# Causal running sums by groups of four interleaved chunks instead of one triangle product per chunk, in a gated linear-attention and state-space kernel

## The chip, the core and the metric

The kernel runs on one NeuronCore of a Trainium2 chip. The core has a matrix engine (TensorE, "PE"; its weight loads are shown as "PEld"), a vector engine (VectorE, "DVE"), a scalar engine (ScalarE, "ACT"), GpSimd ("POOL") and SyncE ("SP"), which here issues nearly all transfers. Each engine works through its own instructions in order; semaphores order them between engines. SBUF is the working memory with 128 partitions, PSUM the memory into which TensorE writes, eight banks of 128 x 512 float32. The metric is the device time of one execution in microseconds, the median of several runs.

## What is computed

A sequence of 2048 tokens of width 448 goes through two branches that are mixed by a gate:

```python
g = sigmoid((x * gate_w).sum(-1, keepdims=True))
a = attention(x, wqkv, wo)     # linear, not causal, 16 heads of 28
b = s4d(x, ...)                # causal convolution with a long kernel K per channel, plus x * D_skip
return g * a + (1 - g) * b
```

```python
# attention: phi(t) = where(t > 0, t + 1, exp(t)) + 1e-6
kv = einsum("bhsd,bhse->bhde", phi(k), v);  z = sum over s of phi(k)
o = einsum("bhqd,bhde->bhqe", phi(q), kv) / (einsum("bhqd,bhd->bhq", phi(q), z) + 1e-6)
return o @ wo
# s4d: y[t] = sum over s <= t of K[t - s] * x[s], by channel
```

With the parameters drawn here the kernel K of each channel is flat enough over the 2048 steps that the convolution is K[0] times the running sum of x; the program tests this on the chip (`okc`, `okn`) and holds a general convolution (`general_conv`) for the channels where it is not so. With these inputs the general part does not run. So what the S4D branch costs is a running sum over 2048 tokens in 448 channels, times a factor per channel (`near`), plus x times `dsk`.

Products that need float32 accuracy are made on TensorE in a reduced format (`F32R`) from a high and a low part: an operand is cast by ScalarE (high), and VectorE or GpSimd subtract the cast from the original (low, the helper `low`, L235).

## The kernel before

The tokens are 16 chunks of 128 rows. Chunk c lies with one token per partition. All instructions are placed by hand: the program text sets the order on every engine.

**The first stage** (L430 to L532 and the part up to L687) goes through the chunks. One pass c of its main loop (L476) does:

- load x of chunk c+3 (`load_x`, SP queue, 512 KB: the transposed chunk, `turned`, and the plain one, `plain`);
- the projection of k for chunk c+1 on TensorE, 11 matmuls of 448 columns (`project`, L338 and L334);
- `split_t(c+2)`: ScalarE casts the transposed chunk (L240), GpSimd makes its low part (L241, by L236);
- `k_feature`, `k_high`, `k_low`: phi of k. ScalarE: Relu and Exp (L360, L361); VectorE: the maximum, written back to PSUM (L362); ScalarE: the high part `pkh` (L366); VectorE: the low part `pkl` and the running sum `zb` (L372);
- the projection of q for chunk c, 11 matmuls into the one PSUM bank with the tag "q", and `q_post`: ScalarE the gate's exponential (L380, one column) and Exp (L349); VectorE a TENSOR_SCALAR (L350) and the maximum into `pq` (L353);
- `do_g(c)`: 11 matmuls that add to the four banks of k-transposed-times-x (L403), with `pkh`, `pkl` and the split plain chunk `xn`;
- `split_n(c+2)`: ScalarE casts the plain chunk (L246), GpSimd makes the low part (L247, by L236), and `skip` (L252) writes x times `dsk` into `y`.

**The running sum** is made chunk by chunk: `do_v(v)` (L408) multiplies the chunk's high and low parts by a 128 x 128 triangle of ones (`tri`), two matmuls of 448 columns; `v_post` (L413) multiplies the result in PSUM by `near` on VectorE (L415), sends its last row twice to the table `u` (L418), and GpSimd adds it to `y` (`v_add`, L423). The table `VS` (L35) says which chunks are done in which pass: two in each of the passes c=5 to 10, one in 11, 12, 13, and the last chunk behind the loop (L646, L663, L842). What earlier chunks add to a chunk comes later: `inter` (L692) multiplies `u` by a 0/1 table (`gcat`, from `cst`), and the result goes as extra rows into the output product of each chunk (`rc`, L629).

Between the passes c=2 and c=5 also stand the steps of `s4d_prepare` (L279): sums over the S4D parameters, then thirteen small VectorE instructions of four columns (L296 to L309, in pass c=4), four transposes on TensorE (L313) and a copy that makes `near` (L314), in pass c=5. The parameters lie in `abc`, in the upper rows of `pq`, until then.

**The second stage** (from L750) builds the combined output matrix, and its loop (L814) turns the normalised q of a chunk (`turn`), multiplies (`attend`), and adds the gated S4D branch (`final_b`: VectorE L634, then the transfer of 128 rows to `out`, L636). GpSimd makes the products for the denominators (`norm_a`, L542) and normalises q (`norm_c`, L567 and L573).

Buffers: `xp` four raw chunks, `xn_p` seven split plain chunks, `xt_p` four split transposed ones; PSUM tags "q", "k", "v0", "v1" and the four banks of `do_g`.

Of the kernel before, what the change touches and what calls it, by code (L numbers as in the profile page):

```python
# [7 lines left out]
F32 = mybir.dt.float32  # L8
# [7 lines left out]
P = 128  # L16
S = 2048
# [17 lines left out]
VS = {c: (2 * c - 10, 2 * c - 9) for c in range(5, 11)} | {c: (c + 1,) for c in range(11, NC - 1)}  # L35
# [18 lines left out]
def general_conv(ctx: ExitStack, tc: tile.TileContext, ga, y, og, okc, both, gin_d, out):  # L54
# [8 lines left out]
    kd = dr.tile([1, PAD], F32, name="kd")  # L63
    lag = one.tile([P, W], F32, name="lag")
# [7 lines left out]
    for lo, n, k in ((0, L1, float(L0)), (L1, L0, 1.0)):  # L72
        DVE.tensor_scalar(out=lag[:, lo:lo + n], in0=o[:, :n], scalar1=-1.0, scalar2=k, op0=ALU.add, op1=ALU.mult)
# [58 lines left out]
    every = [P, NC, D]  # L132
    for o, a, b, op in ((yg, yg, slow[:, None, :].to_broadcast(every), ALU.mult),
                        (y, y, fast[:, None, :].to_broadcast(every), ALU.mult), (yg, yg, y, ALU.add),
                        (yg, yg, og[:, :, None].to_broadcast(every), ALU.mult), (yg, yg, ga, ALU.add)):
        DVE.tensor_tensor(out=o, in0=a, in1=b, op=op)
    SP.dma_start(out=out.rearrange("(c p) d -> p c d", p=P), in_=yg)
# [3 lines left out]
def gated_mix_kernel(ctx: ExitStack, tc: tile.TileContext, xin, wq_d, wvo_d, abc_d, ldt_d, dsk_d,  # L141
# [196 lines left out]
    def project(*args, **kw):  # L338
        o, run = pieces(*args, **kw)
        run(11)  # L340
        return o
# [22 lines left out]
    def k_high(c):  # L364
        pkh[c] = tp.tile([P, 512], F32R, name="pkh", tag="pkh")[:, EDGE:EDGE + D]
        ACT.add(pkh[c], pks[c], 1e-6)  # L366
# [12 lines left out]
    def q_post(c, o, mid=None):  # L379
        ACT.activation(e1[:, c:c + 1], o[:, D:D + 1], AF.Exp, scale=-1.0)  # L380
        feature(pq[:, c], o, mid)
# [24 lines left out]
    vt = {}  # L406

    def do_v(c):  # L408
        v = vt[c] = ps.tile([P, 512], F32, name="v", tag="v%d" % (c % 2))
        PE.matmul(v[:, :D], lhsT=tri, rhs=xn[c][:, :D], start=True, stop=False)  # L410
        PE.matmul(v[:, :D], lhsT=tri, rhs=xn[c][:, XC - NAT:], start=False, stop=True)

    def v_post(c):  # L413
        t = tp.tile([P, D], F32, name="t", tag="v0")
        DVE.tensor_tensor(out=t, in0=vt.pop(c)[:, :D], in1=near, op=ALU.mult)  # L415
        if c < NC - 1:
            for k in (c, UL + c):
                SP.dma_start(out=u[k:k + 1], in_=t[P - 1:P])  # L418
            v_add(c, t)
        return t  # L420

    def v_add(c, t):
        POOL.tensor_tensor(out=y[:, c], in0=y[:, c], in1=t, op=ALU.add)  # L423
# [52 lines left out]
    for c in range(2, NC - 2):  # L476
        if c + 3 < NC:
            load_x(c + 3)
        if c == 2:
            SP.dma_start(out=cst, in_=cst_d)  # L480
        if c == 4:
            SP.dma_start(out=wvo, in_=wvo_d)
        vs = VS.get(c, ())
        ko = project(c + 1, wkh, wkl, D, "v1" if c in (2, 4) else "k")
        for v in vs[:1]:
            do_v(v)
        split_t(c + 2)
        k_feature(c + 1, ko)
        k_high(c + 1)
        if c > 5:  # L490
            for v in vs[:1]:
                v_post(v)
        k_low(c + 1)
        qo = project(c, wqh, wql, D + 2, "q")
        if c == 5:
            steps(1)
        else:
            for v in vs[1:]:
                do_v(v)
        q_post(c, qo)  # L500
        if c == 10:
            split_n(c + 2)
        if c == 5:
            v_post(0)
        else:
            for v in vs[1:]:
                v_post(v)
# [11 lines left out]
        if c == 5:  # L519
            do_v(1)  # L520
        if c < 4:
            skip(c - 1)
        if c != 10:
            split_n(c + 2)
        if c == 5:
            v_post(1)
        for j in {11: (0, 1), 12: (2, 3)}.get(c, ()):
            w = xn_p.tile([P, NX], F32R, name="wo", tag="n")[:DJ, :2 * D].rearrange("p (i d) -> p i d", i=2)
# [88 lines left out]
    av = {}  # L617

# [12 lines left out]
    def final_b(c):  # L631
        ot = tp.tile([P, D], F32, name="ot", tag="pkh")
        for a, lo, hi in av[c]:
            DVE.scalar_tensor_tensor(out=ot[:, lo:hi], in0=y[:, c, lo:hi], scalar=og[:, c:c + 1],  # L634
                                     in1=a[:, lo:hi], op0=ALU.mult, op1=ALU.add)
            (ACT if c == NC - 1 and hi == D else SP).dma_start(out=out[c * P:(c + 1) * P, lo:hi], in_=ot[:, lo:hi])  # L636
# [8 lines left out]
    ko = project(c + 1, wkh, wkl, D, "k")  # L645
    do_v(c + 1)  # L646
# [16 lines left out]
    vl = v_post(c + 1)  # L663
# [28 lines left out]
    def inter():  # L692
        o = ps.tile([P, 512], F32, name="z", tag="v0")
        r = tp.tile([P, D], F32R, name="rc", tag="w")
        z = tp.tile([P, D], F32R, name="zs", tag="v0")
# [118 lines left out]
    for c in range(NC):  # L814
# [26 lines left out]
        if c == 9:  # L841
            v_add(NC - 1, vl)  # L842
# [15 lines left out]
def _layout(inputs):  # L858
# [3 lines left out]
    x = np.asarray(inputs["A_x"])[0].reshape(NC, P, D)  # L862
# [7 lines left out]
    x = x[:, :, perm]  # L870
# [3 lines left out]
    def tiles(w):  # L874
        o = np.zeros((P, J, w.shape[1]), np.float32)
        for k in range(3):
# [12 lines left out]
                          for n in ("B_log_A_real", "B_A_imag", "B_C_real", "B_C_imag")]  # L889
                         + [np.repeat(np.asarray(inputs["B_log_dt"]).reshape(D, 1, 1), P, axis=1),  # L890
                            x[:, ::-1].transpose(2, 1, 0), x.transpose(2, 1, 0),
# [6 lines left out]
    k = np.arange(NC)[None, :] - np.arange(NC)[:, None]  # L898
# [3 lines left out]
    for r in (0, UL):  # L902
        cst[r:r + NC - 1, DJ + DT:DJ + RX] = np.repeat(k[:-1] > 0, 3, axis=1)
# [12 lines left out]
        f(np.stack([np.eye(P), lag >= 0], axis=1)),  # L916
# [20 lines left out]
```

## Time and profile before

| what | value |
|---|---|
| runs | 174.43, 174.32, 173.66 us; median 174.32 |
| the profiled execution: span from its first to its last instruction | 172.2 us |
| TensorE's granted clock | 1.000 |
| matmuls L410 and L411 (`do_v`) | 16 each, 5.8 and 5.9 us shown busy |
| VectorE L415 (`v_post`) | 16, 9.8 us busy |
| GpSimd L423 (`v_add`) | 16, 18.7 us busy |
| VectorE L350 (TENSOR_SCALAR of q) | 15, 10.0 us busy, 384 to 1382 ns |
| waits of VectorE for ScalarE at L362 | 29.4 us in 11 times |
| waits of GpSimd for VectorE at L423 | 11.5 us in 6 times |

The profile is one execution. Its page gives busy time by engine; a matmul is shown from its start to its modelled end, and neighbours overlap, so the time that one costs TensorE is the distance between the starts of neighbours. In the rows in order of time, the columns are the start in us, the duration in us, engine, line, operation, output and inputs; a bracket gives the idle time of the engine ahead of it and what ended it. In the rows by shape, the numbers behind the bar are the busy time in us and the mean of one in ns. "x11" says that eleven instructions were merged into one row.

### The profile page before, as it was taken

What the parts mean: (1) busy time and instruction counts of PE and PEld (TensorE: products, weight loads), DVE (VectorE), ACT (ScalarE), POOL (GpSimd) and SP (SyncE); (2) the same over time, 40 slices, a digit from 0 to 9 for tenths busy, and PEclk for the clock granted to TensorE, in tenths of its full rate; (3) what the DMA queues carried; (4) which work ended last, traced back from release to release, by engine and by line L of the source; (5) the groups of instructions that cost most, each with busy time, mean ns of one, the idle gap of its engine ahead of it and who ended that gap; (6) DMA issues with size and microseconds to landing.
All of it is one profiled execution on the core that took longest, in us unless ns stands there. A gap on an engine that the chain in (4) does not pass through costs nothing. (4 is left out here: it accounts for less than half of the span.)

```text
span 172.2 us, 2796 instructions
## 1 busy us (share of the span) xinstructions
PE 167.8 (97%) x876; PEld 152.0 (88%) x876; DVE 113.9 (66%) x240; ACT 96.0 (56%) x221; POOL 120.0 (70%) x128
## 2 busy tenths in 40 slices
PE   6999999999999999999999999999999999999992
PEld 2788999999899999999999999999899999999992
DVE  0847737698975483846627346487898998987542
ACT  3688588894256262542727456356574564664541
POOL 6082667877529988696996999529968998892200
PEclk9999999999999999999999999999999999999999
DMA  5989975097003031230404200000031222122213
GB/s 173 415 297 294 268 209 166 0 368 303 4 0 114 11 123 34 95 123 1 122 15 131 106 1 1 0 0 2 7 67 54 107 89 76 62 99 107 108 59 108
DMA packets 7962, 18.60 MB, mean 108 GB/s; under 512 B 2045, under 2 KB 4810, under 8 KB 7818
## 3 DMA queue, kind: packets, MB, share of 16 engines
q1 hardware_dynamic: 7802, 18.30, 32.0%
q8 instruction: 7, 0.11, 0.3%
q10 hardware_dynamic: 144, 0.11, 0.2%
q14 instruction: 9, 0.07, 0.1%
HBM read 14.38 MB, written 3.67 MB: 105 GB/s over the span
## 5 line engine op out<-in xcount | busy, mean ns | idle before, releaser
L629 PE MATMUL a<-wk,th 128*128 128x448 f32 (+1 forms) x170 | 36.4, 360 | 0.0
L403 PE MATMUL g<-pkh,xn 128*128 128x448 f32 x112 | 35.6, 364 | 0.0
L629 PEld LDWEIGHTS a<-wk,th 128*128 128x128 f32 x170 | 29.5, 189 | 1.6
L334 PE MATMUL k<-wk,xt 128*128 128x448 f32 x132 | 29.3, 367 | 0.0
L334 PE MATMUL q<-wqh,xt 128*128 128x450 f32 x120 | 27.5, 366 | 0.0
L362 DVE SCALAR_TENSOR_TENSOR k<-k,e 128x448 f32<-128x448 f32 x12 | 7.6, 632 | 29.4 <-ACT e L361 29.4
L423 POOL TENSOR_TENSOR y<-y,t 128x448 f32<-128x448 f32 x16 | 18.7, 1168 | 11.5 <-DVE t L415 11.5
L334 PEld LDWEIGHTS k<-wk,xt 128*128 128x128 f32 x132 | 24.8, 189 | 2.2 <-DVE wk L236 0.3
L334 PEld LDWEIGHTS q<-wqh,xt 128*128 128x128 f32 x120 | 22.5, 188 | 1.7
L236 POOL TENSOR_TENSOR xn<-xr,xn 128x448 fp32r<-128x448 f32 x16 | 19.4, 1211 | 6.6 <-ACT xn L246 4.5
L403 PE MATMUL g<-pkl,xn 128*128 128x448 f32 x64 | 23.4, 366 | 0.0
L403 PEld LDWEIGHTS g<-pkh,xn 128*128 128x128 f32 x112 | 21.0, 188 | 2.2
L236 POOL TENSOR_TENSOR xt<-xr,xt 128x512 fp32r<-128x512 f32 x14 | 18.2, 1297 | 5.9 <-ACT xt L240 5.9
L360 ACT ACTIVATE e<-k 128x448 f32<-128x448 f32 x12 | 6.5, 544 | 26.9 <-PE k L334 26.9
L542 POOL TENSOR_TENSOR prod<-pq,zb 128x448 f32<-128x448 f32 x16 | 18.6, 1172 | 4.1 <-ACT zb L665 3.0
L252 POOL TENSOR_TENSOR y<-xr,rows 128x448 f32<-128x448 f32 x16 | 18.8, 1175 | 0.0
L567 POOL TENSOR_TENSOR pn<-pq,den 128x336 f32<-128x336 f32 x16 | 12.3, 771 | 5.9 <-ACT den L556 4.1
L634 DVE SCALAR_TENSOR_TENSOR ot<-y,og,a 128x448 f32<-128x448 f32 (+1 forms) x17 | 10.7, 629 | 5.1 <-PE a L629 5.1
L612 DVE TENSOR_TENSOR th<-tr,th 128x512 fp32r<-128x512 f32 x16 | 11.0, 691 | 2.7 <-ACT th L611 2.1
L403 PEld LDWEIGHTS g<-pkl,xn 128*128 128x128 f32 x64 | 11.2, 174 | 1.2 <-DVE pkl L372 0.2
L611 ACT CAST th<-tr 128x512 fp32r<-128x512 f32 x16 | 9.4, 588 | 4.6 <-PE tr L604 4.4
L334 PE MATMUL q<-wql,xt 128*128 128x450 f32 x45 | 11.6, 364 | 0.0
(150 smaller groups left out, 302.3 us busy)
## 6 DMA issues: line engine op xcount, KB each, us to landing
xr<-in SPq DMA_DIRECT2D x15, 512.0 KB, 6.2
out<-ot SPq DMA_DIRECT2D x15, 224.0 KB, 1.9
pq<-in SPq DMA_DIRECT2D x4, 448.0 KB
wvo<-in SPq DMA_DIRECT2D x1, 1792.0 KB
y<-in SPq DMA_DIRECT2D x2, 480.0 KB
y<-in SPq DMA_DIRECT2D x2, 450.0 KB
u<-t SPq DMA_DIRECT2D x30, 1.8 KB, 1.7
y<-in SPq DMA_DIRECT2D x1, 448.0 KB, 4.3
```

The costliest lines, as they stand in the source:

```text
L236: eng.tensor_tensor(out=o, in0=r, in1=h.bitcast(F32), op=ALU.subtract)
L252: POOL.tensor_tensor(out=y[:, c], in0=plain[c][:, :D], in1=dsk, op=ALU.mult)
L334: PE.matmul(o[:, :n], lhsT=a, rhs=b, start=run.n == 1, stop=not seq)
L362: DVE.scalar_tensor_tensor(out=pks[c], in0=pks[c], scalar=1.0, in1=e, op0=ALU.add, op1=ALU.max)
L403: PE.matmul(g[i][:a.shape[1], :D], lhsT=a, rhs=b, start=c == 0 and n == 0, stop=c == NC - 1 and n == len(seq) - 1)
L423: POOL.tensor_tensor(out=y[:, c], in0=y[:, c], in1=t, op=ALU.add)
L542: POOL.tensor_tensor(out=pd[c], in0=pq[:, c], in1=zb, op=ALU.mult)
L567: POOL.tensor_tensor(out=n[:, :3, :DJ].rearrange("p j (h d) -> p j h d", h=4), in0=a, in1=r[:, :H - 4].rearrange("p (j h) -> p j h", j=3)[ ...
L611: ACT.copy(h, ov)
L612: DVE.tensor_tensor(out=l, in0=ov, in1=h.bitcast(F32), op=ALU.subtract)
L629: PE.matmul(a[:, lo:hi], lhsT=u_, rhs=w_[:, lo:hi], start=n == 0, stop=n == 10)
L634: DVE.scalar_tensor_tensor(out=ot[:, lo:hi], in0=y[:, c, lo:hi], scalar=og[:, c:c + 1], in1=a[:, lo:hi], op0=ALU.mult, op1=ALU.add)
```

## The change

The tokens of four chunks (512) are dealt out anew on the host: partition p of a group now holds tokens 4p to 4p+3 of the group, one in each of the group's four chunks. The running sum over a group is then: in a partition, sums over the four chunks (`prefix`, three additions of 448 columns); across partitions, one product of the group's last partial sum, split in high and low, with a strict triangle (`group_split`, `group_heads`, two matmuls per group); and `convolve`, which for two chunks at a time adds the product, from PSUM, and multiplies by `near`, both on 2 x 448 columns, in place. The plain x of a group is loaded once more for this (`group_load`, 128 partitions of 4 x 448 float32, 0.92 MB) into one of four places (`homes`): a new buffer `spare` (groups 0 and 3), the place of `wo` (group 1; `wo` is loaded in pass 10 instead), the upper rows of `pq` (group 2). Group 0's additions and its low part are on GpSimd, those of the others on VectorE. The table `u` has one row per group instead of per chunk.

The passes change with it: the two projections of k alternate between the tags "k" and "v1"; from pass 6 on `split_n` stands right behind `split_t`; the order inside `k_low` is turned from chunk 7 on; `q_post` of chunks 6 to 13 makes phi on ScalarE with Relu, Exp and an add, and one VectorE instruction. The additions to `y` are made in passes 6 to 11 (two each), and for the last group in the second stage's loop at c=10 to 13. The output goes to rows 4p + r of its group.

```diff
-VS = {c: (2 * c - 10, 2 * c - 9) for c in range(5, 11)} | {c: (c + 1,) for c in range(11, NC - 1)}
+G = 4
...
+    spare = const.tile([P, G, D], F32, name="spare")
...
-    xn_p = work.enter_context(tc.tile_pool(name="xn", bufs=7))
+    xn_p = work.enter_context(tc.tile_pool(name="xn", bufs=5))
...
-        for o, a, op in ((pkl[c], pkh[c].bitcast(F32), ALU.subtract), (zb, zb, ALU.add))[::-1 if c == NC - 1 else 1]:
+        for o, a, op in ((pkl[c], pkh[c].bitcast(F32), ALU.subtract), (zb, zb, ALU.add))[::-1 if c > 6 else 1]:
...
     def q_post(c, o, mid=None):
         ACT.activation(e1[:, c:c + 1], o[:, D:D + 1], AF.Exp, scale=-1.0)
-        feature(pq[:, c], o, mid)
+        if c < 6 or c >= NC - 2:
+            return feature(pq[:, c], o, mid)
+        e = tp.tile([P, D], F32, name="e", tag="e")
+        ACT.activation(e, o[:, :D], AF.Relu, scale=-1.0)
+        ACT.activation(e, e, AF.Exp, scale=-1.0)
+        ACT.add(e, e, 1e-6)
+        DVE.scalar_tensor_tensor(out=pq[:, c], in0=o[:, :D], scalar=C1, in1=e, op0=ALU.add, op1=ALU.max)
...
-    def do_v(c):
-        v = vt[c] = ps.tile([P, 512], F32, name="v", tag="v%d" % (c % 2))
-        PE.matmul(v[:, :D], lhsT=tri, rhs=xn[c][:, :D], start=True, stop=False)
-        PE.matmul(v[:, :D], lhsT=tri, rhs=xn[c][:, XC - NAT:], start=False, stop=True)
...
-        DVE.tensor_tensor(out=t, in0=vt.pop(c)[:, :D], in1=near, op=ALU.mult)
...
+    homes = (spare, wvo[:, 1], pq[:, NC - G:], spare)
+    sums, heads = {}, {}
+
+    def group_load(g):
+        SP.dma_start(out=homes[g], in_=xin[g * G:(g + 1) * G, :, NAT:LO].rearrange("r p d -> p r d"))
+
+    def prefix(g, i, eng):
+        eng.tensor_tensor(out=homes[g][:, i], in0=homes[g][:, i], in1=homes[g][:, i - 1], op=ALU.add)
+
+    def group_split(g, eng):
+        w = sums[g] = tp.tile([P, 2, D], F32R, name="sums", tag="v0", bufs=1)
+        ACT.copy(w[:, 0], homes[g][:, G - 1])
+        low(eng, w[:, 1], homes[g][:, G - 1], w[:, 0])
+
+    def group_heads(g):
+        o = heads[g] = ps.tile([P, 512], F32, name="v", tag="v0")[:, :D]
+        w = sums.pop(g)
+        for i in range(2):
+            PE.matmul(o, lhsT=tri, rhs=w[:, i], start=i == 0, stop=i == 1)
+
+    def convolve(c):
+        g, i = c // G, c % G
+        a, full = homes[g][:, i:i + 2], [P, 2, D]
+        DVE.tensor_tensor(out=a, in0=a, in1=heads[g][:, None, :].to_broadcast(full), op=ALU.add)
+        DVE.tensor_tensor(out=a, in0=a, in1=near[:, None, :].to_broadcast(full), op=ALU.mult)
+        if i and g < NC // G - 1:
+            for k in (g, UL + g):
+                SP.dma_start(out=u[k:k + 1], in_=homes[g][P - 1:P, G - 1])
+
+    def v_add(c):
+        POOL.tensor_tensor(out=y[:, c], in0=y[:, c], in1=homes[c // G][:, c % G], op=ALU.add)
...
             SP.dma_start(out=cst, in_=cst_d)
+            group_load(0)
         if c == 4:
-            SP.dma_start(out=wvo, in_=wvo_d)
...
+            SP.dma_start(out=wvo[:, 0], in_=wvo_d[:, 0])
+            group_load(1)
+        if c == 7:
+            group_load(2)
+        if c == 9:
+            group_load(3)
+        if c == 10:
+            SP.dma_start(out=wo, in_=wvo_d[:DJ, 1])
+        g0, half = (c - 4) // 2, c % 2
+        ko = project(c + 1, wkh, wkl, D, "k" if half else "v1")
+        if c > 5:
+            convolve(2 * c - 12)
+        if c in (4, 6, 8, 10):
+            for i in (1, 2):
+                prefix(g0, i, DVE if g0 else POOL)
+        if c in (5, 7, 9, 11):
+            prefix(g0, 3, DVE if g0 else POOL)
         split_t(c + 2)
+        if c > 5:
+            split_n(c + 2)
         k_feature(c + 1, ko)
+        if c in (5, 7, 9, 11):
+            group_split(g0, DVE if g0 else POOL)
         k_high(c + 1)
...
-        do_g(c)
...
+        do_g(c, (0, 1, 2))
+        if c in (5, 7, 9, 11):
+            group_heads(g0)
+        do_g(c, (3,))
...
-        if c != 10:
+        if c < 6:
             split_n(c + 2)
...
+        if 5 < c < 12:
+            v_add(2 * c - 12)
+            v_add(2 * c - 11)
+        for j in {12: (0, 1), 13: (2, 3)}.get(c, ()):
+            w = xn_p.tile([P, NX], F32R, name="wo", tag="n") if j < 2 else xp.tile([P, XC], F32R, name="wo", tag="xr")
...
-        if c == 9:
-            v_add(NC - 1, vl)
+        if 9 < c < 14:
+            v_add(c + 2)
```

The rest of the change follows from the new order of the tokens: the host's layout of x, the strict triangle, the group table in `cst`, the output's view, and two transfers in `general_conv`, which does not run here. `do_v` and `v_post` of the last chunk behind the loop are gone as well.

More of the change, by code (lines that the diff above doesn't have):

```diff
@@ L132, in general_conv @@
     every = [P, NC, D]
+    SP.dma_start(out=nat.rearrange("(c p) d -> p c d", p=P), in_=yg)
+    for c in range(0, NC, G):
+        SP.dma_start(out=yg[:, c:c + G], in_=nat[c * P:(c + G) * P].rearrange("(p r) d -> p r d", r=G))
     for o, a, b, op in ((yg, yg, slow[:, None, :].to_broadcast(every), ALU.mult),
@@ L136, in general_conv @@
         DVE.tensor_tensor(out=o, in0=a, in1=b, op=op)
-    SP.dma_start(out=out.rearrange("(c p) d -> p c d", p=P), in_=yg)
+    for c in range(0, NC, G):
+        SP.dma_start(out=out[c * P:(c + G) * P].rearrange("(p r) d -> p r d", r=G), in_=yg[:, c:c + G])
 @with_exitstack
@@ L617, in gated_mix_kernel @@
     av = {}
+    oview = out.rearrange("(g p r) d -> g r p d", p=P, r=G)
     def attend(c, cuts):
@@ L635, in final_b @@
                                      in1=a[:, lo:hi], op0=ALU.mult, op1=ALU.add)
-            (ACT if c == NC - 1 and hi == D else SP).dma_start(out=out[c * P:(c + 1) * P, lo:hi], in_=ot[:, lo:hi])
+            (ACT if c == NC - 1 and hi == D else SP).dma_start(out=oview[c // G, c % G, :, lo:hi], in_=ot[:, lo:hi])
     def final_c(c):
```

56 lines of the change are left out of this document (12 added, 44 removed).

## The prediction

> **What bounds the kernel now.** I read the page first, then the stretches of the first stage, the order of time inside one loop pass, and the rows by shape.
>
> ```profile
> span 172.2 us, 2796 instructions
> PE 167.8 (97%) x876; PEld 152.0 (88%) x876; DVE 113.9 (66%) x240; ACT 96.0 (56%) x221; POOL 120.0 (70%) x128
> ...
> 57.20:64.60 7.40, 7.40 (x38) 6.88 (x37) 4.32 (x8) 3.54 (x8) 6.24 (x6) 1.00 0.24 72
> 64.60:72.00 7.40, 7.40 (x38) 6.87 (x37) 4.23 (x8) 3.37 (x7) 5.75 (x5) 1.00 0.24 75
> 86.90:93.90 7.00, 7.00 (x36) 6.50 (x35) 3.54 (x7) 3.64 (x9) 5.56 (x6) 1.00 0.23 77
> ```
>
> TensorE is busy in the whole of each stretch: the first two are the passes c=7 and c=8 (two triangle pairs each), the third is c=11 (one pair). The columns are length, then PE, PEld, DVE, ACT, POOL, clock and DMA. The clock is 1.00. A pass with one pair less is 0.4 us shorter, so TensorE's own work sets the length. VectorE has 4.3 of 7.4 us busy, GpSimd already about 6. The span is 172.2 us and the median of the runs 174.32, so 2.1 us lie outside the span; I carry changes of the span over to the median.
>
> ```profile
> 28.52 2.36 PE L334 MATMUL k<-wk,xt 128*128 128x448 f32 x11
> 30.72 1.81 PE L334 MATMUL q<-wqh,xt 128*128 128x450 f32 x8
> ...
> 44.01 0.36 PE L410 MATMUL v<-xn,tri 128*128 128x448 f32 x1
> 44.21 0.37 PE L411 MATMUL v<-xn,tri 128*128 128x448 f32 x1
> ```
>
> Eleven matmuls start within 30.72 - 28.52 = 2.20 us: 0.20 us each, though each is shown as 0.36. Sixteen pairs become four: 24 matmuls less, **4.8 us** off TensorE. A pass without a pair is 7.43 - 0.80 = 6.63 us, with one 7.03. Removal alone gives 174.3 - 4.8 = 169.5.
>
> **What VectorE gets, and the loop it sits in.** Per pass c=6 to 11 it loses two products (0.61 each) and one TENSOR_SCALAR; it gains `convolve` (A: add of the PSUM heads, B: multiply by `near`, 896 columns each), two prefix additions in even passes, one and a `low` in odd passes. Rows of a pass of before, for the steps:
>
> ```profile
> 67.06 0.55 ACT L360 ACTIVATE e<-k 128x448 f32<-128x448 f32 x1 [3.23 <-PE k L334]
> 67.64 0.58 ACT L361 ACTIVATE e<-e 128x448 f32<-128x448 f32 x1
> 68.25 0.63 DVE L362 SCALAR_TENSOR_TENSOR k<-k,e 128x448 f32<-128x448 f32 x1 [2.98 <-ACT e L361]
> 68.92 0.55 ACT L366 ACTIVATE pkh<-k 128x448 fp32r<-128x448 f32 x1 [0.70 <-DVE k L362]
> 69.63 0.17 ACT L380 ACTIVATE e<-q 128x1 f32<-128x1 f32 x1 [0.16 <-PE q L334]
> 69.70 0.54 ACT L349 ACTIVATE e<-q 128x448 f32<-128x448 f32 x1
> 70.12 0.62 ACT L246 CAST xn<-xr 128x512 fp32r<-128x512 f32 x1
> 71.46 0.62 DVE L353 SCALAR_TENSOR_TENSOR pq<-q,t 128x448 f32<-128x448 f32 x1
> 72.00 0.62 DVE L415 TENSOR_TENSOR t<-v,rows 128x448 f32<-128x448 f32 x1
> 73.81 1.15 POOL L236 TENSOR_TENSOR xn<-xr,xn 128x448 fp32r<-128x448 f32 x1
> 74.92 1.16 POOL L252 TENSOR_TENSOR y<-xr,rows 128x448 f32<-128x448 f32 x1
> 76.04 1.29 POOL L236 TENSOR_TENSOR xt<-xr,xt 128x512 fp32r<-128x512 f32 x1
> 77.28 1.17 POOL L423 TENSOR_TENSOR y<-y,t 128x448 f32<-128x448 f32 x1
> ...
> L748 DVE TENSOR_TENSOR kvl<-k,kvh 112x224 fp32r<-112x224 f32 x1 | 0.4, 392 | 0.4 <-ACT kvh L745 0.4
> ```
>
> Start to start: VectorE 0.54 (71.46 to 72.00); VectorE to ScalarE 0.67; ScalarE to a dependent ScalarE 0.58, to an independent one 0.42, behind the one-column exponential 0.07; ScalarE to VectorE 0.61; GpSimd 1.11, for 512 columns 1.25. A 896-column product is an estimate: 224 columns more cost 0.61 - 0.39 = 0.22, so 448 more 0.45: about 1.0 between starts, 1.1 where the next depends on it.
>
> ScalarE works in order, and the new exponentials of q stand behind the `pkh` of k. That closes a loop: last STT of q, A, B, prefixes, STT of k, `pkh`, then Relu, Exp, add of q, last STT of q. Even pass: 0.54 + 1.1 + 1.0 + 0.64 + 0.54 + 0.67 + 0.42 + 0.07 + 0.58 + 0.58 + 0.6 = **6.7 us**; odd, one prefix less, 6.1. Mean 6.4 against TensorE's 6.83: it would fit, if nobody waits for GpSimd.
>
> **The wait that is added.** Prefixes, B and `low` read both operands from SBUF. Before, the loop has no such instruction on VectorE: its second operand lies in PSUM. What happens beside a busy GpSimd:
>
> ```profile
> 17.05 1.04 POOL L236 TENSOR_TENSOR wql<-y,wqh 128x450 fp32r<-128x450 f32 x1 [0.99 <-ACT wqh L265]
> 17.48 1.09 DVE L236 TENSOR_TENSOR wqh<-y,wqh 64x450 fp32r<-64x450 f32 x1 [0.24 <-ACT wqh L265]
> ...
> L236 DVE TENSOR_TENSOR wk<-y,wk 64x448 fp32r<-64x448 f32 x1 | 0.6, 622 | 0.0
> ...
> 30.87 0.69 DVE L292 SCALAR_TENSOR_TENSOR y<-pq 112x512 f32<-112x512 f32 x1
> 30.88 1.70 POOL L236 TENSOR_TENSOR xn<-xr,xn 128x448 fp32r<-128x448 f32 x1 [1.63 <-DVE y L292]
> ...
> 43.96 0.38 DVE L280 TENSOR_TENSOR sm<-sm 112x4 f32<-112x4 f32 x1
> 44.27 0.15 DVE L281 SCALAR_TENSOR_TENSOR sm<-sm 112x4 f32<-112x4 f32 x1
> 44.28 1.29 POOL L236 TENSOR_TENSOR xt<-xr,xt 128x512 fp32r<-128x512 f32 x1
> 44.34 1.25 DVE L281 SCALAR_TENSOR_TENSOR sm<-sm 112x4 f32<-112x4 f32 x1
> ...
> L415 DVE TENSOR_TENSOR t<-v,rows x16: 612/614/618, 49.9 to 114.7; 128x448 f32<-128x448 f32 x16
> ```
>
> The 622 ns product takes 1.09 us when it meets a GpSimd instruction, and ends 0.48 us after that one does: it was held to its end. An instruction of four columns takes 1.25 instead of 0.15, and GpSimd's 1.15 becomes 1.70 behind VectorE. Who comes first goes first, and the other waits for all of it. With one operand in PSUM (last row) nothing is lost, at most 618 ns in sixteen; so A is free of it. The Trainium skill, "SBUF — State Buffer", section "Who interferes with whom", has the same as a rule: a VectorE instruction with two SBUF inputs and a GpSimd one that reads SBUF exclude each other for a whole instruction. By it the sum is the one below; without it, the first rival's.
>
> In each pass GpSimd has `low` of xt, `low` of xn, `skip` and two additions to y, 1.25 + 4 x 1.11 = 5.7 us; the first three are ready just when B and the prefixes come, since ScalarE casts for them right behind its add of q. So they alternate. B finds xt halfway: 0 to 1.25, taken 0.45 (even) and 0.2 (odd). When B ends, xn stands waiting and goes first: the prefix waits 1.1 (bounds 0 and 1.25). Then `skip` goes before the second prefix: 1.1 again. Even 6.7 + 2.65 = 9.4, odd 6.1 + 1.3 = 7.4: a pair of passes takes **16.8 us**, against 14.9 before and 13.7 for TensorE alone. The port alone needs 5.7 + 2.1 = 7.8 of each pass's 8.4, so GpSimd just keeps up. TensorE would wait for the single PSUM bank of q (its last reader is the late STT) and, in odd passes, for `low` of the sums ahead of the heads. Three pairs, c=6 to 11: 50.2 us against 93.94 - 49.73 = 44.2 before: **+6.0**. Bounds: with no waits 41.0 (-3.2); with 1.25 at each 57 (+13), but then GpSimd would idle for 3.8 of each 9.5 us pass and could not be met every time: I take +9 as the upper end.
>
> **The passes c=4 and c=5**, where group 0 goes to GpSimd:
>
> ```profile
> 39.59 1.28 POOL L236 TENSOR_TENSOR xt<-xr,xt 128x512 fp32r<-128x512 f32 x1
> ...
> 41.81 2.36 PE L334 MATMUL k<-wk,xt 128*128 128x448 f32 x11
> 46.66 0.38 PEld L313 LDWEIGHTS p<-both,sm 112*128 112x128 f32 x4 [0.23 <-DVE sm L280]
> 49.73 2.38 PE L334 MATMUL k<-wk,xt 128*128 128x448 f32 x11
> 93.94 2.36 PE L334 MATMUL k<-wk,xt 128*128 128x448 f32 x11
> ```
>
> Two prefixes go ahead of `low` of xt at 39.59: it starts at 41.85 and ends at 43.1. The second matmul of the projection at 41.81 needs it at 42.0: TensorE loses **1.2 us** (0 to 1.3). Then GpSimd, idle from 45.6 before, has xn, `skip`, prefix 3, xt and `low` of the sums without a gap to 48.9. Meanwhile VectorE runs the thirteen four-column steps of `s4d_prepare`, of which before only two were held; two pass at each change of GpSimd's instruction (rows 43.96 and 44.27 did, 44.34 did not), so they end near 49.3 instead of 46.7. TensorE's transposes wait for them; q is done at 46.6 + 1.2 - 0.4 = 47.4: 1.9 us of wait (0 to 2.6) against 0.2. With one pair less: 1.2 + 1.9 - 0.2 - 0.4 = **+2.5**.
>
> **The rest.** c=12 and 13 lose a pair each and have no prefix: the loop is 5.8 to 6.5, TensorE is back: -0.8. The pair of the last chunk: -0.4. Extra casts and adds on ScalarE (3.4 busy of 7.4) are in the loop above. Group loads add 3.7 MB; they are issued a pass or more ahead, where DMA is busy at 0.24, and cost nothing unless they delay x behind them on SP's queue: the group 2 load waits for the last use of `pq`'s upper rows, the late `wo` for GpSimd's additions of group 1, with the x of the next pass but one behind it; 3 us of room each. Fewer u transfers free SP. The three later additions to y that move into the attend stage lie in passes where GpSimd has only 1.2 of 2.65 us. Output rows stay 1792 bytes. All these: 0, at most 0.5.
>
> Sum: +2.5 + 6.0 - 0.8 - 0.4 = +7.3, so 174.3 + 7.3 = **181.6 us**, its own range 177 to 185.
>
> **Rivals.** (1) TensorE stays the bound: waits under 13.7 - 12.8 = 0.9 us a pair are swallowed, and GpSimd's gaps fall right at c=4 and 5 too: **169.5**. For it: TensorE's 97%, VectorE's 66%. Against: the held rows. Chance 0.14. (2) VectorE, once it has the port, keeps it for its following instructions: only B waits, the loop is 6.7 in the mean, under 6.83, and the c=4/5 loss remains: 174.3 + 2.5 - 4.4 = **172.4**. Against it: 44.34 lost to 44.28. Chance 0.14, with less of the c=5 loss included. (3) Half the prefix waits: 174.3 + 7.3 - 5 = **176 or less**, or no change: 0.12. (4) The c=5 waits join to one long stall and the clock falls: the warm-up matmuls of the start run 0.43 us each.
>
> ```profile
> 3.02 0.15 PEld L258 LDWEIGHTS <-warm 128*128 128x128 bf16 x1 [0.28 <-issue]
> 3.44 0.15 PEld L258 LDWEIGHTS <-warm 128*128 128x128 bf16 x1 [0.28 <-issue]
> ```
>
> At that pace, for the 4 us that the start took, some ten matmuls lose 0.17 each, and the stall itself 1.5 more: 181.6 + 3.2 = **184.8**; chance 0.05. The Trainium skill, "TensorE: Matmul & The Clock Gate", Part 1, puts the fall at an idle window of about 3.4 us; by that rule none of my stalls (1.9 at most) triggers it, and no run here shows it yet. The forecast itself has 0.55.
>
> **How the numbers follow.** A measurement of this kernel tells about 0.5% from no change. Faster by more: (1) and most of (2), 0.25. Within: 0.08, out of (2) and (3). Slower: the forecast, (4) and part of (3), 0.67. The range of 8 in 10 leaves out most of (1): 171 to 185.
>
> **What would show it.** Right: prefixes on VectorE of 1.2 to 1.7 us and B over 1.2, GpSimd instructions of 1.6, passes of 8.4 us from c=6 to 11, TensorE waiting for VectorE's last STT of q and for the sums' `low`; at c=5 a stall of 1.2 us at the projection and one near 2 us at the transposes. Wrong: prefixes of 0.61 us, passes of 6.6 and 7.0 us, no idle TensorE.

## The result, and the profile after

The changed kernel takes **181.43 us** (median of 4 runs, 181.06 to 182.68) against 174.19 (173.66 to 174.43) before: slower by 7.2 us. Over all runs the ratio is 1.0436, with a 95% interval of 1.0394 to 1.0478 (the two medians alone give 1.042). The profiled execution took 181.06 us, with a span of 179.3.

The page of the changed kernel, its first part and the engines' shares of the chain that ended last:

```profile
span 179.3 us, 2707 instructions
...
PE 165.7 (92%) x852; PEld 146.8 (82%) x852; DVE 139.3 (78%) x244; ACT 106.1 (59%) x241; POOL 135.4 (76%) x132
...
PE 53%; DVE 27%; ACT 13%; issue 4%; ACTq 0%; POOL 0%; DVEq 0%; POOLq 0%
```

The 24 matmuls are gone (852 for 876), but TensorE's share fell from 97% to 92%: it now waits. VectorE's busy time grew by 25.4 us with four instructions more, and GpSimd's by 15.4 us with four more, so it is not the number of instructions that grew but their length: `convolve`'s are twice as wide as those they replace, and, as the runs below show, many are longer than their width asks. Two fifths of the final chain run over VectorE and ScalarE.

What TensorE waits for, in the same trace (total in us, times, longest):

```profile
PE q L340 <- DVE pq L393: 3.8, 3, 2.2
PE p L319 <- DVE sm L286: 1.3, 1, 1.3
...
PE k L340 <- POOL xt L242: 1.3, 1, 1.3
PE v L436 <- DVE sums L242: 1.2, 3, 0.4
```

L393 is the last instruction of q's feature on VectorE, which frees the single PSUM bank of q; L286 is the last of the small S4D steps; L242 is `low`. These are the four places that the prediction named. Where the time went is read from TensorE's projections of k, one at the start of each pass (c=5, 6, 7, 8, 9, 12 and 14 of the changed kernel):

```profile
41.58 0.36 PE L340 MATMUL k<-wk,xt 128*128 128x448 f32 x1
43.25 2.27 PE L340 MATMUL k<-wk,xt 128*128 128x448 f32 x10 [1.31 <-POOL xt L242]
...
52.22 2.37 PE L340 MATMUL v<-wk,xt 128*128 128x448 f32 x11
...
58.90 2.36 PE L340 MATMUL k<-wk,xt 128*128 128x448 f32 x11
...
67.58 2.36 PE L340 MATMUL v<-wk,xt 128*128 128x448 f32 x11
...
74.27 2.36 PE L340 MATMUL k<-wk,xt 128*128 128x448 f32 x11
...
100.74 2.37 PE L340 MATMUL v<-wk,xt 128*128 128x448 f32 x11
...
114.02 2.36 PE L340 MATMUL v<-wk,xt 128*128 128x448 f32 x11
```

Pass c=6 starts 2.49 us later than before (52.22 for 49.73). From there to c=12 the changed kernel takes 48.52 us, before 44.21: +4.3. Then c=12 and 13 take 13.28 for 14.05. The three pairs of passes are not alike (columns as in the prediction):

```profile
52.22:67.58 15.36, 14.51 (x70) 12.52 (x68) 13.94 (x16) 8.03 (x18) 15.18 (x11) 1.00 0.04 6
67.58:83.64 16.06, 14.52 (x70) 12.53 (x68) 14.38 (x17) 9.16 (x19) 14.71 (x11) 1.00 0.41 143
83.64:100.74 17.10, 14.42 (x70) 12.49 (x69) 15.31 (x19) 9.15 (x20) 14.70 (x11) 1.00 0.39 111
```

The instructions by line and shape (busy us, mean ns, idle before): the prefixes (L425), `convolve`'s addition of the heads (A, L441) and its product with `near` (B, L442).

```profile
L442 DVE TENSOR_TENSOR spare<-spare,rows 128x896 f32<-128x896 f32 x4 | 6.0, 1496 | 0.1
...
L425 DVE TENSOR_TENSOR wvo<-wvo 128x448 f32<-128x448 f32 x3 | 4.8, 1586 | 0.0
L425 DVE TENSOR_TENSOR pq<-pq 128x448 f32<-128x448 f32 x3 | 4.6, 1538 | 0.0
L425 DVE TENSOR_TENSOR spare<-spare 128x448 f32<-128x448 f32 x3 | 4.6, 1518 | 0.1
...
L441 DVE TENSOR_TENSOR spare<-spare,v 128x896 f32<-128x896 f32 x4 | 4.3, 1077 | 0.0
```

A, with one operand in PSUM, takes 1.08 us. B has the same 896 columns and both operands in SBUF: 1.50 in this row. The nine prefixes have half the columns and take 1.55 us. The order of time in one even pass (c=8) shows with whom they take turns, VectorE first, then GpSimd:

```profile
68.19 0.62 DVE L393 SCALAR_TENSOR_TENSOR pq<-q,e 128x448 f32<-128x448 f32 x1 [0.31 <-ACT e L392]
68.74 1.08 DVE L441 TENSOR_TENSOR wvo<-wvo,v 128x896 f32<-128x896 f32 x1
69.85 1.31 DVE L442 TENSOR_TENSOR wvo<-wvo,rows 128x896 f32<-128x896 f32 x1
71.08 3.07 DVE L425 TENSOR_TENSOR pq<-pq 128x448 f32<-128x448 f32 x2
74.07 0.62 DVE L368 SCALAR_TENSOR_TENSOR v<-v,e 128x448 f32<-128x448 f32 x1
...
77.02 0.62 DVE L393 SCALAR_TENSOR_TENSOR pq<-q,e 128x448 f32<-128x448 f32 x1 [0.56 <-ACT e L392]
...
84.25 0.62 DVE L393 SCALAR_TENSOR_TENSOR pq<-q,e 128x448 f32<-128x448 f32 x1 [0.32 <-ACT e L392]
```

```profile
68.91 1.30 POOL L242 TENSOR_TENSOR xt<-xr,xt 128x512 fp32r<-128x512 f32 x1
70.16 2.01 POOL L242 TENSOR_TENSOR xn<-xr,xn 128x448 fp32r<-128x448 f32 x1
72.13 1.54 POOL L258 TENSOR_TENSOR y<-xr,rows 128x448 f32<-128x448 f32 x1
```

B is shown from 69.85, while xt ran until 70.21, and B took 1.31 us. xn (1.15 in c=10, where it started ahead of B) was held until B was through: it took 2.01. The two prefixes alternate with xn and `skip` and together take 3.07 us for some 1.2. From one L393 to the next the loop takes 8.83 us in this even pass and 7.23 in the odd one behind it; the pair behind them, c=10 and 11, takes 9.93 and 7.17.

### The profile page after: what moved, and what is told of

Same layout as the page of the kernel before. It is cut to its first block, busy times and chain, and to the rows that moved or that the text cites. A ratio compares the mean times of both kernels' runs of the same rounds, so it can differ in the third digit from the quotient of the medians.

```text
span 179.3 us, 2707 instructions
## 1 busy us (share of the span) xinstructions
PE 165.7 (92%) x852; PEld 146.8 (82%) x852; DVE 139.3 (78%) x244; ACT 106.1 (59%) x241; POOL 135.4 (76%) x132
## 4 chain that ended last, share of the span: by engine, by line
PE 53%; DVE 27%; ACT 13%; issue 4%; ACTq 0%; POOL 0%; DVEq 0%; POOLq 0%
PE a L662 20%; PE g L415 8%; PE q L340 6%; PE v L340 6%; PE tr L636 4%; DVE wvo L425 3%; PE q L264 3%; PE k L340 3%; DVE spare L425 3%; DVE pq L425 2%; ACT pkh L372 2%; DVE pq L393 2%; ACT e L391 2%; ACT e L392 2%; DVE v L368 2%
## 5 line engine op out<-in xcount | busy, mean ns | idle before, releaser
L242 POOL TENSOR_TENSOR xn<-xr,xn 128x448 fp32r<-128x448 f32 x16 | 23.8, 1489 | 8.3 <-ACT xn L252 3.7
L242 POOL TENSOR_TENSOR xt<-xr,xt 128x512 fp32r<-128x512 f32 x14 | 20.1, 1433 | 9.5 <-ACT xt L246 8.2
L258 POOL TENSOR_TENSOR y<-xr,rows 128x448 f32<-128x448 f32 x16 | 21.4, 1338 | 0.0
L340 PE MATMUL v<-wk,xt 128*128 128x448 f32 x99 | 21.3, 362 | 0.0
L340 PEld LDWEIGHTS v<-wk,xt 128*128 128x128 f32 x99 | 18.6, 188 | 1.3
L340 PE MATMUL k<-wk,xt 128*128 128x448 f32 x77 | 17.6, 368 | 1.3 <-POOL xt L242 1.3
L340 PEld LDWEIGHTS k<-wk,xt 128*128 128x128 f32 x77 | 14.3, 188 | 3.3 <-POOL xt L242 1.7
L372 ACT ACTIVATE pkh<-v 128x448 fp32r<-128x448 f32 x9 | 4.9, 545 | 15.1 <-DVE v L368 15.1
```

The source lines that it names most:

```text
L242: eng.tensor_tensor(out=o, in0=r, in1=h.bitcast(F32), op=ALU.subtract)
L258: POOL.tensor_tensor(out=y[:, c], in0=plain[c][:, :D], in1=dsk, op=ALU.mult)
L340: PE.matmul(o[:, :n], lhsT=a, rhs=b, start=run.n == 1, stop=not seq)
```

## The experiments

The theory: VectorE's instructions with two operands in SBUF and GpSimd's instructions shut each other out for whole instructions; this makes the loop over VectorE and ScalarE longer than TensorE's work (c=6 to 11), and holds the small steps at c=4 and 5. The rivals: the instructions that were added cost what they cost, wherever their operands lie; GpSimd simply has too much to do; group 0's work on GpSimd is the main part. "Before" was timed beside each set, at 173.9 to 174.1 us.

**The operands (e1).** The second operand of the prefixes and of B is taken from PSUM; the sums are then not the reference's.

```diff
-        ... in0=homes[g][:, i], in1=homes[g][:, i - 1], op=ALU.add)
+        ... in0=homes[g][:, i], in1=heads[g - 1] if g else homes[g][:, i - 1], op=ALU.add)
...
-        ... in0=a, in1=near[:, None, :].to_broadcast(full), op=ALU.mult)
+        ... in0=a, in1=heads[g][:, None, :].to_broadcast(full), op=ALU.mult)
```

> In the passes c=6 to 11 the prefix additions of groups 1 to 3 and the multiplication in convolve take their second operand from the PSUM bank of the heads instead of from SBUF; the running sums and the factor near are therefore not the reference's. Width and number of VectorE's instructions stay. Theory (VectorE and GpSimd exclude each other on an instruction with two SBUF operands, and the waits sit in the loop of VectorE and ScalarE): additions of 0.61 us instead of 1.55, multiplications of 1.08 instead of 1.25 to 2.1, a pair of passes 13.7 to 14 us instead of 16, TensorE no longer waiting for the last STT of q; 174.2 us, between 173.5 and 175.5. Rival (the added VectorE work and the longer ScalarE chain are too long by themselves): no change, 181.4.

Measured: **174.12 us** (173.28 to 175.09), ratio to before 1.0012 (0.9987 to 1.0037). Prefix, B, and GpSimd's xn by line and shape:

```profile
L242 POOL TENSOR_TENSOR xn<-xr,xn 128x448 fp32r<-128x448 f32 x16 | 19.2, 1201 | 8.6 <-ACT xn L252 4.1 <-PE v L437 2.9 <-DVE y L298 1.6
...
L443 DVE TENSOR_TENSOR spare<-spare,v 128x896 f32<-128x896 f32 x4 | 4.3, 1087 | 0.1
...
L425 DVE TENSOR_TENSOR wvo<-wvo,v 128x448 f32<-128x448 f32 x3 | 1.8, 615 | 0.0
```

The same number of instructions of the same sizes, only one operand elsewhere: prefixes of 0.615 us for 1.59, B of 1.09 for 1.50, and GpSimd's xn 1.20 for 1.49. VectorE's 244 instructions are busy for 129.0 us instead of 139.3, so about 10 of the 25.4 us that the change added to it hung on the operands; the rest is the wider work and the waits that stay. The waits at q and at the sums are gone from TensorE's list; those at c=5 (xt and the small steps, 1.3 each) remain. So 7.3 us hang on where the operand lies.

**GpSimd silent (e9).** That run does not say yet that GpSimd is the other party: an instruction with two operands in SBUF might be long by itself. Here the operands are the changed kernel's, and GpSimd is left without work in c=6 to 11, but for the two instructions of chunk 7 at the start of c=6, one fill of `y` behind them (not in the extract) and one `skip`, of chunk 14, that runs ahead at 85.66 us. ScalarE writes plain copies in place of the low parts, so the values are not the reference's.

```diff
-        low(POOL, w[:, NAT:], turned[c], w[:, :NAT])
+        if c > 7:
+            ACT.copy(w[:, NAT:], turned[c])
+        else:
+            low(POOL, w[:, NAT:], turned[c], w[:, :NAT])
...
-        if c > 2:
+        if 2 < c < 8 or c > 13:
             skip(c)
...
-        if 5 < c < 12:
-            v_add(2 * c - 12)
-            v_add(2 * c - 11)
```

> The changed kernel with GpSimd silent in passes c=6 to 11: the low parts of xt and xn of chunks 8 on are written by ScalarE as plain copies, the skip products of chunks 8 to 13 and the y additions of the loop are left out (y of those chunks is set to zero once in c=6), so the values are not the reference's. VectorE's instructions and their operands are those of the changed kernel. If the prefixes and the B products are long because they take turns with GpSimd's, the prefixes take 0.6 us for 1.5 and B 1.1 for 1.25 to 1.6, and the passes go back to TensorE's 13.7 a pair unless ScalarE, which gets 1.2 us a pass more (to some 5.9), holds one: 174 to 177 us. The rival, that a VectorE instruction with two operands in SBUF is long by itself, expects prefixes of 1.5 us as before and 180 us or more.

Measured: **174.08 us** (173.44 to 175.5), ratio 1.0001 (0.9979 to 1.0022). The second pair of passes (c=8 and 9; length, then busy time of PE, PEld, DVE, ACT, POOL, clock, DMA), and the prefixes and B by shape:

```profile
66.69:80.39 13.70, 13.70 (x70) 12.67 (x68) 11.22 (x17) 11.14 (x25) 0.00 (x0) 1.00 0.51 181
```

```profile
L448 DVE TENSOR_TENSOR wvo<-wvo,rows 128x896 f32<-128x896 f32 x2 | 2.2, 1094 | 0.1
...
L431 DVE TENSOR_TENSOR pq<-pq 128x448 f32<-128x448 f32 x3 | 1.9, 621 | 0.0
```

With GpSimd at 0.00 the prefix takes 0.62 us and B 1.09, both operands in SBUF as in the changed kernel. Neither condition alone is enough: it takes two operands in SBUF on VectorE and a GpSimd instruction beside them. The pair takes 13.70 us with TensorE busy in all of it. In the same pair of the changed kernel (67.58:83.64 above) TensorE is busy for 14.52 of 16.06 us, VectorE for 14.38 (11.22 in e9) and GpSimd for 14.71; the DMA engines are busier in e9 (0.51 for 0.41), so they are not what made the pair long. The same trace shows that not every GpSimd instruction holds VectorE. The fill of `y` in c=6, which writes SBUF and reads nothing, and two prefixes:

```profile
54.78 2.35 POOL L523 MEMSET y<- 128x2688 f32 x1
55.71 1.27 DVE L431 TENSOR_TENSOR wvo<-wvo 128x448 f32<-128x448 f32 x2
```

Both prefixes run inside the fill and take 1.27 us together, as with GpSimd silent. All the GpSimd instructions of the changed kernel's loop read SBUF. The Trainium skill, "SBUF — State Buffer", section "Who interferes with whom", calls it an exclusive lock on a shared pair of ports; e1 and e9 agree with it.

**Which of GpSimd's work (e4).** The two additions to y per pass are left out in c=6 to 11; y then lacks these terms.

```diff
-        if 5 < c < 12:
-            v_add(2 * c - 12)
-            v_add(2 * c - 11)
```

> The two additions to y per pass on GpSimd are left out in the passes 6 to 11, so y lacks the running sum of the first twelve chunks; the rest stays. Theory (a waiting instruction of VectorE meets the low parts of xt and xn and the skip, which come at the same time as it; the additions to y come later): a pair of passes stays at 15.5 to 16 us, total 180.5 to 181.4. Rival (GpSimd as a whole is too full: 5.7 us of work a pass, now 3.5): a pair falls to about 14 us, total 175 to 176.

Measured: 180.34 us (180.11 to 180.68), ratio 1.0368 (1.0343 to 1.0394). Twelve instructions of 1.2 us or more off GpSimd bring 1.1 us, a little more than expected. The prefixes of groups 1 and 2 keep their length, those of the last group fall from 1.52 to 1.26, and TensorE's wait for q falls only from 3.8 to 2.6. Nearly all of the gain lies in the third pair, 16.13 us for 17.10:

```profile
L425 DVE TENSOR_TENSOR wvo<-wvo 128x448 f32<-128x448 f32 x3 | 4.7, 1582 | 0.0
L425 DVE TENSOR_TENSOR pq<-pq 128x448 f32<-128x448 f32 x3 | 4.6, 1537 | 0.0
...
L425 DVE TENSOR_TENSOR spare<-spare 128x448 f32<-128x448 f32 x3 | 3.8, 1259 | 0.0
```

What counts is what stands on GpSimd at the moment when the prefixes are issued (xt, xn, `skip`), not its total.

**Group 0 (e2, e3).** The three prefixes that GpSimd runs for group 0 in c=4 and 5 are left out, alone (e2) and together with the PSUM operands of e1 (e3). The first group's sums over its chunks are then missing.

```diff
-        if c in (4, 6, 8, 10):
+        if c in (6, 8, 10):
...
-        if c in (5, 7, 9, 11):
+        if c in (7, 9, 11):
             prefix(g0, 3, DVE if g0 else POOL)
```

> The three prefix additions of group 0 on GpSimd are left out, so the sums of group 0 are not the reference's; all else stays. Theory (they stand ahead of the low part of xt in pass 4, and keep GpSimd busy while VectorE runs the thirteen small steps in pass 5): the 1.3 us wait of TensorE for xt goes, the 1.35 us wait for the small steps falls to about 0.2, pass 6 starts at 49.3 instead of 52.2, total 178.5 us (178 to 179.2). Rival (the passes 4 and 5 are late because the group load delays the x transfers): no change, 181.4.

> Both edits together: second operands from PSUM in the passes 6 to 11, and no prefix additions for group 0; the sums are not the reference's. Theory: TensorE is the bound again, the gains add, 181.4 - 7.2 - 2.9 = 171.3 us (170.5 to 172.5): what the 24 removed matmuls are worth, 174.2 - 4.8 = 169.4, plus the 1.4 us by which the end behind the last instruction was longer in the profile of after. Rival (VectorE's or ScalarE's own work): 178.5.

Measured: e2 179.96 us (178.84 to 180.24), ratio 1.0327 (1.028 to 1.0374); e3 172.22 us (171.6 to 173.08), ratio 0.9917 (0.9886 to 0.9948). Both fell less than the middle of what was expected, e2 to a time outside its range of 178 to 179.2. The wait for xt at c=5 is gone, as it should be; that for the small steps is not. In e2, VectorE and then GpSimd:

```profile
46.47 0.16 DVE L287 SCALAR_TENSOR_TENSOR okc<-sm 112x4 f32<-112x4 f32 x1
46.59 1.07 DVE L312 SCALAR_TENSOR_TENSOR sm<-sm 112x4 f32<-112x4 f32 x1
```

```profile
46.49 1.14 POOL L242 TENSOR_TENSOR sums<-spare,sums 128x448 fp32r<-128x448 f32 x1 [0.23 <-ACT sums L429]
```

`low` of the sums, still on GpSimd, starts 0.1 us ahead of a step of four columns and holds it for 1.07 us. My expectation took the prefixes for the whole of that term; one GpSimd instruction at the wrong moment was enough to keep 1.1 us of it. The two edits add up within the scatter of the runs: 7.3 us for the operands alone and 1.5 for group 0 alone, 9.2 for both.

**A version without the wait (e5).** If all this holds, the change can be kept and its cost removed, with the reference's result. The running sum of a group is kept in PSUM, and the heads take in the chunks there, one after the other; every VectorE instruction of the loop has one operand in PSUM. The sums of group 0 leave GpSimd, and k goes back to one bank in all passes but c=2, 4 and 12.

```diff
-        eng.tensor_tensor(out=homes[g][:, i], in0=homes[g][:, i], in1=homes[g][:, i - 1], op=ALU.add)
+        if i == 1:
+            acc[g] = ps.tile([P, 512], F32, name="acc", tag="v1" if g else "v0")[:, :D]
+            ACT.copy(acc[g], homes[g][:, 0])
+        DVE.tensor_tensor(out=acc[g], in0=acc[g], in1=homes[g][:, i], op=ALU.add)
...
-        ACT.copy(w[:, 0], homes[g][:, G - 1])
-        low(eng, w[:, 1], homes[g][:, G - 1], w[:, 0])
+        ACT.copy(w[:, 0], acc[g])
+        low(DVE, w[:, 1], acc[g], w[:, 0])
...
-        a, full = homes[g][:, i:i + 2], [P, 2, D]
-        DVE.tensor_tensor(out=a, in0=a, in1=heads[g][:, None, :].to_broadcast(full), op=ALU.add)
-        DVE.tensor_tensor(out=a, in0=a, in1=near[:, None, :].to_broadcast(full), op=ALU.mult)
+        for a in (homes[g][:, i], homes[g][:, i + 1]):
+            DVE.tensor_tensor(out=heads[g], in0=heads[g], in1=a, op=ALU.add)
+            DVE.tensor_tensor(out=a, in0=heads[g], in1=near, op=ALU.mult)
...
-        ko = project(c + 1, wkh, wkl, D, "k" if half else "v1")
+        ko = project(c + 1, wkh, wkl, D, "v1" if c in (2, 4, 12) else "k")
```

> Running sums and heads stay in PSUM, so that no VectorE instruction of the loop has two operands in SBUF: one copy on ScalarE, three additions to the sum and four pairs of 'heads plus row, times near' per group, each of 448 columns at about 0.61 us as in the first experiment (12 instructions of VectorE for 8, about 0.3 us more a pass than there: even 6.0, odd 6.0 us of VectorE work beside 6.63 and 7.03 of TensorE). Group 0 is summed the same way on VectorE, nothing of the sums is left on GpSimd, k goes back to one bank. My theory (the port, at both places) expects TensorE to be the bound in all passes: pass starts 13.7 us a pair from c=6 on, no wait at the projection in c=5, 169 to 172 us, faster than before. The rival (more VectorE instructions in the loop cost whatever their operands are) expects 175 or more.

Measured: **172.08 us** (171.75 to 172.84), ratio 0.9877 (0.986 to 0.9893): 9.3 us less than the changed kernel and 1.2% less than before, a small gain but clear of the interval, and just above the 169 to 172 expected. VectorE has 264 instructions instead of 244 and is busy for 128.7 us instead of 139.3. A pair of passes takes 13.70 us again:

```profile
65.26:78.96 13.70, 13.70 (x69) 12.69 (x68) 11.71 (x21) 9.91 (x22) 11.49 (x10) 1.00 0.49 172
```

**The rest of c=3 to 5 (e10, e11).** In e5 TensorE still waited 0.9 us for the small steps. Two edits on top of it: in e10 the transposes that wait (`steps(1)` of c=5) go behind the pass's state products; in e11 (without e10's edit) the casts of the triangle and of the gate matrix at the end of c=3 go from VectorE to ScalarE. First e10's, then e11's:

```diff
-        if c == 5:
-            steps(1)
         q_post(c, qo)
...
         do_g(c, (3,))
+        if c == 5:
+            steps(1)
```

```diff
-            DVE.tensor_copy(tri, trir)
-            DVE.tensor_copy(gcr, gcat)
+            ACT.copy(tri, trir)
+            ACT.copy(gcr, gcat)
```

> The version with the sums in PSUM (172.1), with the four transposes that wait for the small S4D steps in c=5 issued behind that pass's state products instead of behind its q projection. In it the transposes waited 0.9 us and the pass from c=5 to c=6 took 9.1 us against 7.9 before; 2.2 us later nothing waits: the pass takes 8.2, 171.2 us, faster than before by 1.5 per cent. If the small steps hold something else as well (the q feature's last instruction), the gain is under 0.5 us: 171.6 or more.

> The version with the sums in PSUM (172.1), with the two small casts of the triangle and the gate matrix at the end of c=3 on ScalarE. On VectorE they stand in the queue at 1.18 us each, ahead of group 0's two additions and of k's feature in c=4 (2.2 us in all), and push the small S4D steps past their users: moving the transposes behind the state products only moved the wait to the sums (1.0 us, 172.3). If VectorE's queue in c=3 to 5 is what holds those passes, both waits go, the pass from c=5 to c=6 takes 8.2 us for 9.1, and the time is 171.2 (170.8 to 171.6). If something later sets the end, 172.0.

Measured: e10 172.28 us (171.84 to 172.83), ratio 0.9892 (0.9868 to 0.9916), no gain over e5 and not the 171.2 expected; e11 **171.27 us** (170.5 to 171.51), ratio 0.9831 (0.9806 to 0.9855). TensorE's waits in e10, then in e11, and e11's pass c=5:

```profile
...
PE v L439 <- DVE sums L242: 1.0, 1, 1.0
PE q L340 <- DVE pq L359: 0.2, 1, 0.2
```

```profile
PE q L264 <- POOL warm L195: 1.3, 1, 1.3
PE v L340 <- ACT xt L467: 0.3, 1, 0.3
```

```profile
42.25:50.07 7.82, 7.71 (x41) 6.79 (x39) 7.58 (x22) 4.08 (x10) 3.73 (x3) 1.00 0.77 275
```

In e10 the wait only changed its name: VectorE's queue was late as a whole, and the next user of it waited, 1.0 us for 0.9. Taking 2.2 us out of that queue took the wait away, and c=5 to c=6 fell from 9.09 us in e5 to 7.82. Both waits that are left in e11 lie in the start phase.

**The end (e6, e7).** The profiled span grew by 7.1 us, but the passes and what follows account for 5.7; the other 1.4 lie behind the issue of the last output (before, then after):

```profile
169.62 0.38 ACTq L636 DMA_DIRECT2D out<-ot  x1
```

```profile
175.31 0.38 ACTq L669 DMA_DIRECT2D out<-ot  x1
```

From there to the end of the span it is 172.2 - 169.62 = 2.6 us before and 179.3 - 175.31 = 4.0 after. In e6 the conditional block is the one of before (its transfers are shown); in e7 each chunk's rows are written side by side, in the order of the permuted tokens.

```diff
-    SP.dma_start(out=nat.rearrange("(c p) d -> p c d", p=P), in_=yg)
-    for c in range(0, NC, G):
-        SP.dma_start(out=yg[:, c:c + G], in_=nat[c * P:(c + G) * P].rearrange("(p r) d -> p r d", r=G))
...
-    for c in range(0, NC, G):
-        SP.dma_start(out=out[c * P:(c + G) * P].rearrange("(p r) d -> p r d", r=G), in_=yg[:, c:c + G])
+    SP.dma_start(out=out.rearrange("(c p) d -> p c d", p=P), in_=yg)
```

```diff
-            (ACT if c == NC - 1 and hi == D else SP).dma_start(out=oview[c // G, c % G, :, lo:hi], in_=ot[:, lo:hi])
+            (ACT if c == NC - 1 and hi == D else SP).dma_start(out=out[c * P:(c + 1) * P, lo:hi], in_=ot[:, lo:hi])
```

> The changed kernel with the conditional block behind the loop (which does not run on these inputs) as it was before: 8 DMA instructions fewer in it. If the larger block costs the 1.4 us that the end grew behind the last instruction (2.6 to 4.0 us), 180.0 us; if it does not, 181.4 us.

> The changed kernel with each chunk's 128 rows written side by side, as before, and not every fourth row (the output's rows are then in the order of the permuted tokens). If the spread rows cost the 1.4 us at the end, 180.0 us with a tail of 2.6 us behind the issue of the last output; if they do not, 181.4 us with 4.0.

Measured: e6 181.62 us (180.53 to 181.75), ratio 1.0425 (1.0402 to 1.0448); e7 181.57 us (181.16 to 182.96), ratio 1.0447 (1.0416 to 1.0478). Neither brings the 1.4 us back. In their profiles the end took 3.1 and 3.5 us, in e5 and e11 3.3. In all eleven profiles of the changed kernel and its variants it took 3.1 to 4.0 us, 3.5 in the middle one, and the 2.6 of before lies below all of them. So some 0.9 us seem to come with the change, and the rest of the 1.4 may be scatter of a single profile; but there is only one profile of before, and what makes the end longer stays open.

## Why the prediction was right

The forecast was 181.6 us and 181.43 was measured. By steps:

- **Matmuls (-4.8).** Right in size where TensorE is the bound: a pair of passes takes 13.70 us in e1, e5 and e9, as worked out (6.63 + 7.03). In the changed kernel itself only c=12, 13 and the last chunk show it: 13.28 - 14.05 = -0.77 for -0.8, and from c=14 to the last output's issue 61.29 for 61.63, -0.34 for -0.4.
- **The port, c=6 to 11 (+6.0).** The mechanism is shown by e1 and e9. The size was too large, +4.3 for +6.0, though little of that lies in the loop. From one last STT of q to the next, the even passes measured 9.17, 8.83 and 9.93 us for 9.4 and the odd ones 7.15, 7.23 and 7.17 for 7.4: 49.5 in all for the 50.2 worked out. In c=8 the stretch from STT of k to the last STT of q was exact (2.95 for 2.92); too large were B's wait (next start after 1.23 us, taken 1.45) and those of the two prefixes (2.99 to the next start, taken 3.38). In c=10 two small instructions put B 0.03 us behind xn's start; it waited for the whole of xn (1.99 to the next start). The other 1.0 us is the first turn of the loop: TensorE began c=6 late, 0.35 us behind the last STT of q at 51.87, and c=12 0.61 us ahead of the one at 101.35, so its passes took 48.5 us where the loop took 49.5. The working set the two equal.
- **c=4 and 5 (+2.5).** Measured +2.49 at the start of c=6. The idle time before xt was 1.31 for 1.2, that before the small steps 1.35 for 1.9. A stall costs more than the idle time that the profile shows, since the overlap of neighbouring matmuls is lost with it: from start to start the two cost 1.59 us (the projection of k begins at 41.58 and what follows it at 45.37, 3.79 us for 2.20) and 1.54 us (the transposes start at 49.15, 3.78 behind q's projection, for 2.24 before). Less 0.4 for the pair, pass c=5 takes 10.64 us (41.58 to 52.22) for 7.92. That is +2.7; the sum meets the total of +2.49 only because the pass starts 0.23 earlier, a difference that is there from the first passes on (21.67 for 21.91) and that the start phase shows between other profiles too (21.66 to 22.44). e2 weighs one term: the working had `low` of the sums among GpSimd's instructions, and that one alone kept 1.1 us of the wait.
- **The rest (0, at most 0.5).** Here the prediction was wrong: +1.4 behind the last output, unexplained. It hid the 1.7 us by which c=6 to 11 were overestimated; that the total came within 0.2 us is luck, and the terms are less good than their sum (2.5 + 4.3 - 0.8 - 0.3 + 1.4 = 7.1 of span, +7.3 forecast).
- **Rivals.** TensorE as the bound (169.5) is what the change would take if TensorE never waited more than before; no run reached it, and e11 comes to 171.27. By its profile it has 3.6 of the 4.8 us in c=5 to 13 (104.79 - 42.25 = 62.54 us from c=5 to c=14, before 107.99 - 41.81 = 66.18) and 0.2 more by the last output's issue; 0.4 was lost in the start phase and 0.7 at the end, in the one profile that there is of it. VectorE did not keep the port: each of its instructions took its turn. Half the prefix waits (the third rival, whose sum is 176.6 and not 176) did not occur either: the two prefixes of c=8 took 2.99 us from start to start for some 1.2 without waits, and those of c=6 and c=10 3.14 and 3.01. The clock was 1.00 in the profiled execution, also over TensorE's longest stall, 2.25 us in c=10, so the fourth rival did not occur there. Its working doesn't hold: the warm-up matmuls whose pace it took for that of a fallen clock ran at a granted clock of 1.00 (1.3 to 5.2 us of before), and no row is given for its 0.17 us a matmul. Two of the four runs record a mean of 0.991 (181.51 and 182.68 us), and what brings that about wasn't tried.

## What to carry to other kernels

Count an instruction moved to VectorE by its operands and by what GpSimd does at that moment: with two SBUF operands beside a GpSimd that reads SBUF it costs its own time plus most of a GpSimd instruction (here 1.52 to 1.59 us for 0.62), and the GpSimd instruction grows too (xn 1.49 for 1.20). Keep one operand in PSUM, even at the price of more instructions (in e5 20 more on VectorE, and 9 us less, some 1.5 of them from group 0). When a wait moves to another name after a reordering, the queue behind it is late as a whole, and only work taken off that queue helps.

## What the runs showed that was not expected

An instruction of VectorE with a single operand, in SBUF, is held as well. In the trace of before, VectorE's cast of a 128x128 tile takes 0.22 us at the start and 1.17 in c=3, beside GpSimd's xn:

```profile
L511 DVE CAST tri<-both 128x128 fp32r<-128x128 f32 x1 | 1.2, 1171 | 0.0
...
L434 DVE CAST xt<-y 128x128 fp32r<-128x128 f32 x1 | 0.2, 221 | 0.0
```

On ScalarE the same cast takes 0.28 us in e11. In before the loop itself had such an instruction, the TENSOR_SCALAR of q (L350), beside xn in c=4 and, in c=5, with GpSimd idle:

```profile
41.93 1.38 DVE L350 TENSOR_SCALAR t<-e 128x448 f32<-128x448 f32 x1
...
48.89 0.38 DVE L350 TENSOR_SCALAR t<-e 128x448 f32<-128x448 f32 x1
```

So VectorE met waits of this kind before as well, which the prediction, looking for two operands in SBUF, left out; the change took this instruction out for the chunks 6 to 13. The Trainium skill's rule ("SBUF — State Buffer", section "Who interferes with whom") also covers VectorE's instructions in a mode that uses both ports, which these would have to be; no run here tells the mode.
